# Attention mixed with a long convolution on one core: table exponentials ahead of the sines, a quarter of x transposed by DMA, operands padded to 128 rows, zero products, a new order

## The chip, the core and the metric

The kernel runs on one core of a Trainium2 chip. The metric is the device time of one execution in microseconds (us). The engines of the core each work through a queue of their own: TensorE (PE; its weight loads are listed as PEld), VectorE (DVE), ScalarE (ACT), GpSimd (POOL) and SyncE (SP). DMAs are issued from the queues of SP, ACT and POOL.

## The reference, cut to what matters

```python
x = A_x                                              # 1 x 2048 x 448, bf16
g = sigmoid((x * gate_w).sum(-1, keepdims=True))
q = heads(x @ wq)                                    # 16 heads of 28
k = x @ wk;  v = x @ wv                              # one head of keys and values for all
p = softmax(q @ k.T * 28 ** -0.5)                    # 16 x 2048 x 2048
a = join(p @ v) @ wo
dt = exp(log_dt)
P = exp(dt * (A_re + 1j * A_im) * arange(2048))      # 448 channels x 256 modes x 2048
K = einsum("dn,dnl,dn->dl", C, P, dt * B).real       # one filter of 2048 taps per channel
b = causal_convolution(x, K) + x * Dskip
return g * a + (1 - g) * b
```

## The kernel before, in words

**Attention.** Scores are computed transposed, 128 keys by 512 queries a tile, 1024 tiles in all. They go in sets of three tiles and two tiles in turn (410 sets). `qk` (in `main`) issues a set's score products, either with the tiles of three heads beside each other in TensorE's rows (`row`, L1260) or one whole-array product per tile against the masked copy qM (`full`, L1269). ACT takes the exponential of a whole set in one instruction (L1293), out of five of the eight PSUM banks into a ring of 15 tiles in SBUF. `pv` (L1311) multiplies four tiles with the values and sums in bank 6; a column of ones beside the values gives the softmax's denominators. After 64 tiles, `norm` divides, and after four such groups `outp` and `fold` add the gated result to O in SBUF.

**Convolution.** `prep_params` turns the parameters into tables: on ACT `dt` (L801), a half and a whole sine (L833, L836), and six table exponentials, one of A_re times dt (L845) and five of its multiples (L849, `mq`). `masters` and `tables` build, on DVE and per block of 32 channels, tables of powers (14 blocks); `kgen` makes the filter taps of a block by small products, and writes them to DRAM (KP). `tload` reads them back as Toeplitz blocks of 512 KB (224 loads on SP's queue, L1068), and `conv` multiplies them with x in the order of U (L1092).

**The front.** `loads` brings x in four quarters (two DMAs each), the weights with 112 rows, the parameters, four of them transposed by the DMA, A_re plain. `prep_x` transposes every quarter of x by 16 products with the identity (L665) in four PSUM banks, copies them out on ACT (L676) and DVE (L678), projects the keys (L684), takes their largest magnitude (L691), and copies the keys out on ACT (L694). From the magnitudes comes Wb (L721, L722), which shifts the scores; `qproj` projects the queries of one group (L891, L897, L900, L903). The first scores need all of that. `warm` products with the identity (L522) keep TensorE's clock. Quarters 1 to 3 of the transposed x are parked in DRAM (XS). U is filled by eight copies on POOL (L617) and one DMA that shifts it by 16 columns. O's zeros come by DMA from a zero tile (zO) once the transposed x that lies in O has been used.

**The order.** `Prog` collects all operations with their dependencies and an estimate of each one's duration, and `schedule` lays out every engine's queue by a greedy list rule: earliest start first, priorities `pr` next; before the first softmax exponential the longest chain to it (shifted by the hand-set RANK) decides. `after` adds edges that are only for the order: it places the table exponentials behind the softmax exponentials of sets 2, 4, 6, 8, 10 and 12 (pexp). TWICE repeats the score products of the first tile in two-tile sets from set 10 to 23. PSUM banks 5 and 7 are lent to everything that is not scores or value sums (POOL = (7, 5)).

Of the kernel before, what the change touches and what calls it, by code (L numbers as in the profile page):

```python
# [28 lines left out]
FLIP = (0, 2, 3, 4, 5)  # L29
# [8 lines left out]
SIN2PI = 6.2831850  # L38
SQ = 1.0 / math.sqrt(DH)
# [31 lines left out]
class Op:  # L71
    __slots__ = ("i", "eng", "fn", "ns", "lat", "deps", "pr", "lock", "unlock", "slot", "ndma",
                 "count", "vc", "end", "comm", "extra", "mode", "ni", "done", "waits", "sb", "tl", "tfree", "frees")


class Prog:
# [6 lines left out]
    BLOCK, FIRST, FETCH, IDLE, NEED = 256, 192, 5900.0, 3300.0, .015  # L83
    HALF = (21000.0, 32000.0, 1.8)
    HEAD = 0.4
    RANK = {142: -3000, 102: -1500, 107: 1500, 188: -700, 28: -1500, 23: -3000, 121: -3000, 33: 1500, 57: 1500, 93: -700, 181: -700}
    POOL = (7, 5)
    AHEAD = 1500.0
    SLACK = {"pe": 400.0, "dve": 150.0}

    def __init__(self, nc, es):
        self.nc, self.es = nc, es
        self.ops = []
        self.lastw = {}
        self.readers = {}
        self.slots = {}
        self.commops = {}
        self.after = {}
        self.convs = []

# [36 lines left out]
    def dma(self, pairs, desc, slot, rd=(), wr=(), pr=0, eng="sp", slow=False, extra=0, flip=False, cost=None):  # L137
# [11 lines left out]
        o.slot, o.ndma, o.extra = slot, len(pairs), extra  # L149
# [16 lines left out]
    def schedule(self):  # L166
# [27 lines left out]
        self.clock = {e: {} for e in ENG}  # L194
        block = [0.0, 0.0]
# [11 lines left out]
        while done < n:  # L207
# [53 lines left out]
            if e == "pool" and o.slot is None:  # L261
                for d in reversed(order[e]):
                    if ops[d].slot is None:
                        o.deps[d] = 1
                        break
            o.done = True
# [26 lines left out]
            if o.slot is not None:  # L293
                free[e] = r + self.ISSUE[e] * o.ndma
# [3 lines left out]
            else:  # L298
# [5 lines left out]
                if e == "pool":  # L304
                    held.append((r, free[e]))
            o.end = end
# [25 lines left out]
        return order  # L332

# [36 lines left out]
    def emit(self, block):  # L370
# [11 lines left out]
        for e in ENG:  # L382
# [3 lines left out]
            def body(x, e=e):  # L386
                for i in self.order[e]:
# [7 lines left out]
                    else:  # L395
                        r.then_inc(sem[e], 1)
                if e == "sp":
# [26 lines left out]
TWICE = 24  # L424


class Kernel:
# [26 lines left out]
    def alloc(self):  # L454
# [43 lines left out]
        self.XS = nc.dram_tensor("XS_scratch", (3 * DT * XQ,), BF).ap()  # L498
        self.R = nc.dram_tensor("R_scratch", (16 * 4 * 512,), F32).ap()

    def consts(self):
# [23 lines left out]
        self.warm = lambda n, b, ns: pg.op("pe", lambda e: warm(e, n, b), ns, rd=["id"], wr=[("b", b)], pr=-3)  # L525
# [3 lines left out]
        for _ in range(2):  # L529
            self.wd.append(len(pg.ops))  # L530
            self.warm(1, 3, 430)
        pm(V(self.Wm, 0, P), 0.0, 100, ["Wm"], 1)
# [20 lines left out]
    def loads(self):  # L553
# [4 lines left out]
        def lx(q):  # L558
            pg.dma([(bass.AP(tensor=self.xst.h, offset=h * self.xst.rs + q * 4 * D, ap=[[2 * self.xst.rs, 64], [D, 4], [1, D]]),
                     dram(x, (1024 * h + 256 * q) * D, [[D, 64], [64 * D, 4], [1, D]])) for h in range(2)],  # L560
                   (512, 896), f"x{q}", wr=[("xst", q)])
# [5 lines left out]
        def lraw(k):  # L567
            if k in FLIP:
                pg.dma([(raw.v(0, P, k * 1024, [[D, 2], [1, D]]), dram(ins[names[k]], 0, [[NM, D], [1, NM]]))],
                       (448, 512), f"raw{k}", wr=[("raw", k)], pr=0 if k < 2 else 0.2, flip=True, cost=1700)  # L570
# [13 lines left out]
        pg.dma([(wst.v(0, DT, 0, [[1, 4 * D]]), dram(ins["A_wq"], 0, [[4 * D, DT], [1, 4 * D]]))],  # L584
               (112, 3584), "wq", wr=["wqs"])
        pg.dma([(wks.v(0, DT, 112, [[1, 112]]), dram(ins["A_wv"], 0, [[112, DT], [1, 112]])),
                (wks.v(0, DT, 224, [[1, 4]]), dram(ins["gate_w"], 0, [[4, DT], [1, 4]]))],
               (224, 224), "wv", wr=["wvs"])
        lraw(1)
        pg.op("pool", lambda e: e.tensor_copy(self.Wk.v(0, DT, 0, [[32, 16], [1, DH]]),  # L590
                                             wks.v(0, DT, 0, [[DH, 4], [0, 4], [1, DH]])), 640, rd=["wks"], wr=["Wk"])
        pg.op("dve", lambda e: e.tensor_copy(self.Wq.v(0, DT, 0, [[512, NT], [32, 4], [1, DH]]),
                                             wst.v(0, DT, 0, [[16 * DH, NT], [DH, 4], [1, DH]])), 390, rd=["wqs", "Wq"], wr=["Wq0"], sb=True)
        pg.op("dve", lambda e: e.tensor_copy(self.Wq.v(0, DT, 128, [[512, NT], [32, 12], [1, DH]]),
                                             wst.v(0, DT, 4 * DH, [[16 * DH, NT], [DH, 12], [1, DH]])), 480, rd=["wqs"], wr=["Wq"], sb=True, pr=1)
        self.wvc = len(pg.ops)
        pg.op("dve", lambda e: e.tensor_copy(self.Wv.v(0, DT, 0, [[32, 4], [1, DH]]), wks.v(0, DT, 112, [[DH, 4], [1, DH]])),
              180, rd=["wvs"], wr=["Wv"], sb=True, pr=0.1)
        pg.op("dve", lambda e: e.tensor_copy(self.Wv.v(0, DT, 28, [[32, 4]]), wks.v(0, DT, 224, [[1, 4]])),
              100, rd=["wvs"], wr=["Wvg"], sb=True, pr=0.1)  # L600
# [12 lines left out]

        for q in range(4):
            for j in (0, 2):
                u = 15 - 4 * q - j
                pg.op("pool", lambda e, u=u: e.tensor_copy(  # L617
                    self.U.v(0, P, u - 1, [[32, D], [1, 2]]),
                    self.xst.v(0, P, (16 - u) * D, [[1, D], [-D, 2]])), 1080,
# [31 lines left out]
    def prep_x(self):  # L651
# [3 lines left out]
        for q in range(4):  # L655
            xT, xo = self.xq(q)
            t4, o4 = self.bank(4 + 2 * (q % 2))
            X = ("b", 4 + 2 * (q % 2))
            for T in (2, 0, 3, 1):
# [744 lines left out]
```

## Time and profile before

| | us |
|---|---|
| median of the runs shown (508.69, 508.8, 510.62) | 508.8 |
| the profiled execution | 507.82 |
| its span, first to last instruction | 505.8 |
| busy: ACT / DVE / PE / POOL | 485.6 / 451.6 / 451.5 / 163.7 |
| first softmax exponential starts | 20.61 |
| last softmax exponential ends | 497.99 |
| granted TensorE clock, mean | 0.959 |

The profile's page gives busy time by engine, the span in 40 slices with the granted clock (PEclk, in tenths of full speed), the costliest groups of instructions with the idle time ahead of them and what ended it, and the DMA issues. The trace behind it can be asked for a timeline of one engine, for the waits, and for busy time and clock in any stretch. A busy time says how full an engine is, not that it sets the end; what sets it is read from the idle time of the others ahead of their instructions.

### The profile page before, as it was taken

How to read it: one execution, taken by the hardware profiler on the slowest of the kernel's cores; microseconds unless marked ns; L12 is line 12 of the kernel's file. 1: busy time of each engine (PE TensorE's matmuls, PEld its weight loads, DVE VectorE, ACT ScalarE, POOL GpSimd, SP SyncE). 2: the span in 40 equal slices, each digit the busy share in tenths (PEclk: the TensorE clock that was granted, in tenths of full speed). 3: DMA queues.
4: the chain of work that ended last, by engine and by line, in shares of the span. 5: the costliest groups of instructions: out<-in, count | busy, mean ns of one | idle time of the engine just before them, and what ended most of it. 6: DMA issues, size and time to landing. Idle time of an engine off the chain costs nothing.

```text
span 505.8 us, 18926 instructions
## 1 busy us (share of the span) xinstructions
PE 451.5 (89%) x8474; PEld 197.9 (39%) x8474; DVE 451.6 (89%) x825; ACT 485.6 (96%) x438; POOL 163.7 (32%) x304
## 2 busy tenths in 40 slices
PE   8888788897889899989898999999898999999895
PEld 5413131342434344334344444343344443444463
DVE  7999999999999999999999999999999999423434
ACT  5999999999999999999999999999999999999883
POOL 8800223252233424215205525225133525051001
PEclk9959977999999999989999999999999999999988
DMA  8987408959889788988998999999996999999922
GB/s 209 238 65 117 98 7 246 346 185 318 299 267 309 231 281 266 359 296 257 371 296 241 348 358 305 340 366 292 358 324 231 373 374 372 370 372 386 361 74 45
DMA packets 115730, 138.45 MB, mean 274 GB/s; under 512 B 48841, under 2 KB 55402, under 8 KB 115650
## 3 DMA queue, kind: packets, MB, share of 16 engines
q1 hardware_dynamic: 105872, 127.82, 78.4%
q0 software_dynamic: 8768, 9.31, 7.0%
q8 instruction: 66, 1.08, 0.9%
q10 hardware_dynamic: 1010, 0.12, 0.2%
q14 instruction: 14, 0.11, 0.1%
HBM read 125.41 MB, written 5.22 MB: 258 GB/s over the span
## 4 chain that ended last, share of the span: by engine, by line
DVE 52%; ACT 34%; PE 10%; issue 2%; DMA 1%; SPq 1%
ACT expT L1293 33%; DVE tab L985 8%; DVE tab L997 5%; DVE tab L996 5%; DVE tab L1007 4%; DVE tab L994 4%; DVE tab L995 4%; DVE tmp L1003 3%; PE psS L1269 2%; PE psB L1311 2%; DVE msq L928 2%; DVE cst L1107 2%; PE psS L1260 2%; DVE seedz L932 1%; DVE mbf L948 1%
## 5 line engine op out<-in xcount | busy, mean ns | idle before, releaser
L1293 ACT ACTIVATE expT<-psS 128x1536 bf16<-128x1536 f32 (+1 forms) x410 | 466.6, 1338 | 6.4 <-PE psS L1260 4.1
L1269 PE MATMUL psS<-qM,kT 128*128 128x512 bf16 (+2 forms) x464 | 127.7, 370 | 13.0 <-ACT expT L1293 12.3
L1260 PE MATMUL psS<-qT,kT 29*128 29x512 bf16 (+2 forms) x702 | 86.1, 374 | 25.6 <-ACT expT L1293 22.2
L1311 PE MATMUL psB<-expT,vaug 128*32 128x512 bf16 (+2 forms) x1152 | 106.3, 378 | 0.4 <-issue 0.2
L143 POOL DMA_DIRECT2D KP_scratch<-kstg x112 | 61.6, 558 | 70.1 <-DVE kstg L1047 42.8
L985 DVE TENSOR_TENSOR tab<-tab,mbf 128x512 bf16<-128x512 bf16 (+3 forms) x56 | 64.5, 1153 | 0.0
L1311 PEld LDWEIGHTS psB<-expT,vaug 128*32 128x32 bf16 x1152 | 27.8, 94 | 79.3 <-issue 75.0
L143 POOL DMA_DIRECT2D rdenB<-R_scratch x56 | 28.5, 515 | 67.5 <-DMA R_scratch<-denT 46.8
L1260 PEld LDWEIGHTS psS<-qT,kT 29*128 29x128 bf16 x702 | 22.1, 92 | 71.2 <-ACT expT L1293 56.2
L1269 PEld LDWEIGHTS psS<-qM,kT 128*128 128x128 bf16 x464 | 30.2, 99 | 50.4 <-ACT expT L1293 33.4
L143 POOL DMA_DIRECT2D qM<-qT x64 | 32.2, 511 | 31.7 <-DVE qT L903 15.4
L996 DVE TENSOR_TENSOR tab<-tab 128x128 bf16<-128x128 bf16 (+4 forms) x70 | 41.8, 597 | 0.0
L997 DVE TENSOR_TENSOR tab<-tab 128x128 bf16<-128x128 bf16 (+4 forms) x70 | 41.6, 594 | 0.0
L1092 PE MATMUL psX<-T,U 128*32 128x128 bf16 (+3 forms) x1472 | 34.9, 222 | 0.8 <-issue 0.7
L1007 DVE TENSOR_TENSOR tab<-tab,tmp 128x4096 bf16<-128x4096 bf16 x14 | 31.9, 2278 | 0.1
L994 DVE TENSOR_TENSOR tab<-tab,mbf 128x4096 bf16<-128x4096 bf16 x14 | 32.0, 2285 | 0.0
L995 DVE TENSOR_TENSOR tab<-tab,mbf 128x4096 bf16<-128x4096 bf16 x14 | 31.9, 2280 | 0.0
L1092 PE MATMUL psS<-T,U 128*32 128x128 bf16 (+7 forms) x1248 | 29.6, 220 | 1.9 <-issue 1.0
L1092 PEld LDWEIGHTS psX<-T,U 128*32 128x32 bf16 (+3 forms) x1472 | 24.9, 94 | 13.6 <-issue 10.2
L143 POOL DMA_DIRECT2D denT<-acc x14 | 10.0, 716 | 60.8 <-DVE acc L1166 56.0
L1092 PEld LDWEIGHTS psS<-T,U 128*32 128x32 bf16 (+7 forms) x1248 | 20.4, 93 | 15.9 <-issue 11.9
L928 DVE TENSOR_TENSOR msq<-seedz 128x512 f32<-128x512 f32 (+3 forms) x50 | 26.2, 523 | 0.1
(164 smaller groups left out, 537.1 us busy)
## 6 DMA issues: line engine op xcount, KB each, us to landing
T<-KP_scratch SPq DMA_DIRECT2D x170, 512.0 KB, 8.6
U<-KP_scratch SPq DMA_DIRECT2D x40, 512.0 KB, 9.2
tab<-KP_scratch SPq DMA_DIRECT2D x14, 512.0 KB, 9.9
rdenB<-R_scratch POOLq DMA_DIRECT2D x56, 64.0 KB
qM<-qT POOLq DMA_DIRECT2D x64, 32.0 KB, 4.9
tab<-in_A_x_dram SPq DMA_DIRECT2D x8, 224.0 KB, 3.5
O<-cst SPq DMA_DIRECT2D x1, 1792.0 KB, 9.2
KP_scratch<-kstg POOLq DMA_DIRECT2D x112, 16.0 KB, 4.4
```

The costliest lines, as they stand in the source:

```text
L143: return [e.dma_start(o, i, **kw) for o, i in pairs]
L985: vo(lambda e, dst=dst, src=src, mri=mri: e.tensor_tensor(dst, src, mri, ALU.mult), 4 * n, done + mk(lv), [kr, ki, tk])
L994: vo(lambda e, src=src, mi=mi, tv=tv: e.tensor_tensor(tv, src, mi, ALU.mult), 2 * n, done + mk(lv), [tk])
L995: vo(lambda e, dst=dst, src=src, mr=mr: e.tensor_tensor(dst, src, mr, ALU.mult), 2 * n, done + mk(lv), [kr, ki, ("gap", s)])
L996: vo(lambda e, dc=dc, tc=tc: e.tensor_tensor(dc[0], dc[0], tc[1], ALU.subtract), n, [tk, kr], [kr])
L997: vo(lambda e, dc=dc, tc=tc: e.tensor_tensor(dc[1], dc[1], tc[0], ALU.add), n, [tk, ki], [ki])
L1007: vo(lambda e: e.tensor_tensor(tab.v(0, P, FM, [[4, 1024], [1, 4]]), tab.v(0, P, lo + 124, [[CG, 32], [-4, 32], [1, 4]]), rho.v(0, P, 0, [ ...
L1092: r = e.matmul(ps.v(32 * j, 32 - 2 * n, 128 * k, [[1, 128]]), self.U.v(0, P, (4 * gi + j) * 32 + 2 * n, [[1, 32 - 2 * n]]), tbuf.v(0, P, t ...
L1260: r = e.matmul(self.psS.v(0, P, 512 * b + o, [[1, n]]), kT.v(32 * h, DH + 1, 128 * kt, [[1, 128]]), qT.v(32 * h, DH + 1, 512 * (i % 2) + q ...
L1269: r = e.matmul(self.psS.v(0, P, 512 * b + o, [[1, n]]), kT.v(0, P, 128 * kt, [[1, 128]]), self.qM.v(0, P, (i % 2) * XQ + 512 * h + qo, [[1 ...
L1293: pg.op("act", lambda e: e.activation(expT.v(0, P, 512 * es[0], spread(es, n)), self.psS.v(0, P, 512 * bs[0], spread(bs, n)), AF.Exp, scal ...
L1311: r = e.matmul(self.psB.v(32 * h, 32, qo, [[1, n]]), vaug.v(0, P, 32 * kt, [[1, 32]]), expT.v(0, P, 512 * ring[t] + o, [[1, n]]), start=(k ...
```

## The change

- A_re is also transposed by the DMA (FLIP has 1), so its eight products and its PSUM group go. The six table exponentials stand ahead of the sines in ACT's queue, before the softmax begins; the sine table is loaded behind them, and the order edges pexp go.
- Quarter 2 of x comes transposed by two DMAs (DQ) from rows of 512 columns, of which 448 count; its 16 products and four copies go. It is also loaded plain, for U, behind the parameters, and its two copies into U stand behind the softmax exponentials of sets 6 and 11 (UF). Its columns have another order (`cols`), as have the reciprocals of its gate, now seven small ones for one.
- x, Wk, Wv, Wq and the gate's weights lie on 128 rows (three of 128 and one of 64, zeros below) instead of 112. Wk, Wv and the gate's weights are issued on ACT's queue, in two DMAs each.
- The transposes of x use two PSUM banks in place of four; the quarters go in the order 0, 1, 3, 2; fewer copies are on ACT (XA); the keys of quarter 0 are copied out on DVE (KD).
- Zero products: `idle` watches, while the order is made, how much of the last 3.4 us TensorE works, and where it is below 0.49 between 36 and 440 us puts products of the identity with a zero column into bank 6's sum (`filler`). There are 19 of them. TWICE goes from 24 to 40, three warm products follow each of the first four sets, and bank 5 is lent out after those.
- The scheduler's numbers change (HEAD, RANK, SLACK and others), some priorities, and with them the order on every engine.

```diff
-FLIP = (0, 2, 3, 4, 5)
+FLIP = (0, 1, 2, 3, 4, 5)
...
+XA = ((0, 1), (0, 3), (1, 3), (2, 1), (3, 1), (3, 2), (3, 3))
+KD = (0,)
+GX = 3
+DQ = (2,)
+NA, NB, ND = 4, 4, 4
+UF = range(6, 26, 5)[:2 * len(DQ)]
+QO = (0, 1, 3, 2)
...
-    POOL = (7, 5)
+    POOL = (7,)
+    LOW, SPAN, FILL = .49, 3413.0, (36000.0, 440000.0)
...
+    def idle(self, order, free, r, o):
+        a, span = self.act, self.SPAN
+        busy = sum(x for e, x in a[-60:] if e > r - span)
+        k = 0
+        if self.part < 15 and self.FILL[0] < r < self.FILL[1] and busy < self.LOW * span:
+            k = max(0, int(min((r - free - 60.0) / 218.0, (self.LOW * span - busy) / 215.0 + 1.0)))
...
-TWICE = 24
+TWICE = 40
...
+            if q in DQ and not y:
+                xT, xo = self.xq(q)
+                pg.dma([(xT.v(0, P, xo + 256 * h, [[512, 4], [1, 256]]), dram(x, (1024 * h + 256 * q) * D, [[D, 256], [1, 512]]))
+                        for h in range(2)], (1024, 512), f"w{q}", wr=self.xk(q), flip=True, cost=2500)
+                return
...
-        lx(0)
-        pg.dma([(wks.v(0, DT, 0, [[1, 112]]), dram(ins["A_wk"], 0, [[112, DT], [1, 112]]))], (112, 224), "wk", wr=["wks"])
-        lx(1)
-        lraw(0)
-        lx(2)
-        lx(3)
...
-        lraw(1)
+        lx(QO[0])
+        pg.dma(rows(wks, 0, ins["A_wk"], DH), (448, 56), "wk", wr=["wks"], eng="act", cost=150)
+        lx(QO[1])
+        lraw(1)
+        lraw(0)
+        pg.dma(rows(wst, 0, ins["A_wq"], D), (448, 896), "wq", wr=["wqs"], cost=1500)
+        lx(QO[2])
+        lx(QO[3])
+        pg.dma(rows(wks, 4 * DH, ins["A_wv"], DH), (448, 56), "wv", wr=["wvs"], eng="act", cost=150)
...
         def texp(e):
-            r = e.activation(dtp, d1, AF.Copy, scale=1.0 / TWO_PI)
-            e.preload_act_table(AF.Sin)
-            return r
+            return e.activation(dtp, d1, AF.Copy, scale=1.0 / TWO_PI)
...
+        pg.op("act", lambda e: e.activation(t(2), t(0), AF.Exp), 950, rd=[K(0)], wr=[K(2)], pr=-1)
+
+        def modulus(e, lv):
+            r = e.activation(self.mq.v(0, P, lv * W2, [[32, 2], [64, NC], [1, 32]]), tc(0), AF.Exp, scale=-2.0 * 2 ** lv)
+            if lv == 4:
+                e.preload_act_table(AF.Sin)
+            return r
...
-            for k, x in enumerate((2, 4, 6, 8, 10, 12)):
-                if s == x:
-                    pg.after[self.pexp[k]] = len(pg.ops) - 1
...
+            if s < ND:
+                x = len(pg.ops) - 1
+                for k in range(3):
+                    pg.after[len(pg.ops)] = x
+                    self.warm(1, 5, 218, 0.6)
...
+        pg.filler = lambda e: e.matmul(self.psB.v(0, P, 0, [[1, 512]]), self.ident.v(0, P, 0, [[1, P]]), vaug.v(0, P, 29, [[0, 512]]),
+                                       start=False, stop=True, tile_position=(0, 0), skip_group_check=True)
```

More of the change, by code (lines that the diff above doesn't have):

```diff
@@ L194, in schedule @@
         self.clock = {e: {} for e in ENG}
+        self.fill, self.act, self.part = {}, [], 15
         block = [0.0, 0.0]
@@ L265, in schedule @@
                         break
+            if e == "pe":
+                npe += 2 * self.idle(order[e], free[e], r, o)
             o.done = True
@@ L332, in schedule @@
         return order
+    def idle(self, order, free, r, o):
[4 more added lines that the diff above has]
+            k = max(0, int(min((r - free - 60.0) / 218.0, (self.LOW * span - busy) / 215.0 + 1.0)))
+        if k:
+            self.fill[order[-1]] = k
+            a.append((r, 215.0 * k))
+        a.append((r + o.ns, min(o.ns, 213.0 * o.ni / 8.0 if o.mode == "q" else o.ns)))
+        self.part = self.parts.get(o.i, self.part)
+        return k
     def clocks(self, o, order, tot):
@@ L396, in body @@
                         r.then_inc(sem[e], 1)
+                    for _ in range(self.fill.get(i, 0)):
+                        self.filler(x)
                 if e == "sp":
@@ L654, in prep_x @@
         sm = self.small
-        for q in range(4):
+        nb = 0
+        for iq, q in enumerate(QO):
             xT, xo = self.xq(q)
-            t4, o4 = self.bank(4 + 2 * (q % 2))
-            X = ("b", 4 + 2 * (q % 2))
-            for T in (2, 0, 3, 1):
-                b = (4 * q + T) % 4
+            t4, o4 = self.bank((4, 3, 2, 5)[iq])
+            X = ("b", (4, 3, 2, 5)[iq])
+            for T in (2, 0, 3, 1) if q not in DQ else ():
+                b = nb % 2
+                nb += 1
                 t, o = self.bank(b)
@@ L726, in prep_x @@
         self.q0 = q0 = [o.i for o in pg.ops[self.wb:] if o.eng == "dve"][-1]
-        pg.after[self.wvc] = pg.after[self.wvc + 1] = q0
+        pg.after[self.wqc] = q0
+        for k in range(NB):
+            pg.after[len(pg.ops)] = q0 - 1
+            self.warm(1, 3, 218, 0.6)
         self.q1 = len(pg.ops)
```

219 lines of the change are left out of this document (123 added, 96 removed).

## The prediction

> **What bounds the kernel now.** I read the page's busy shares first, then its clock row and its costliest groups, then ScalarE's (ACT) timeline, last the stretch table.
>
> ```profile
> PE 451.5 (89%) x8474; PEld 197.9 (39%) x8474; DVE 451.6 (89%) x825; ACT 485.6 (96%) x438; POOL 163.7 (32%) x304
> ...
> PEclk9959977999999999989999999999999999999988
> ...
> L1293 ACT ACTIVATE expT<-psS 128x1536 bf16<-128x1536 f32 (+1 forms) x410 | 466.6, 1338 | 6.4 <-PE psS L1260 4.1
> ```
>
> ACT is busy 96% of the span, 466.6 us of it with the 410 softmax exponentials, which this change keeps one for one. They form a stream from 20.61 to 497.99 us. So the span is four terms: the front before the first exponential (20.6), the exponentials, what else stands in their stream (idle 6.4, and other ACT work), and the end behind the last (505.8 - 498.0 = 7.8). Whoever wants time must take it from the front, the fill or the end.
>
> The fill, in ACT's timeline (start, duration, line, operation, idle before it):
>
> ```profile
> 19.46 0.69 ACT L694 ACTIVATE kT<-psS,small 128x512 bf16<-128x512 f32 x1
> 20.04 0.68 ACT L694 ACTIVATE kT<-psB,small 128x512 bf16<-128x512 f32 x1
> 20.61 3.70 ACT L1293 ACTIVATE expT<-psS 128x1536 bf16<-128x1536 f32 x3
> 24.17 0.98 ACT L845 ACTIVATE T<-T 128x896 f32<-128x896 f32 x1
> 25.01 1.05 ACT L1293 ACTIVATE expT<-psS 128x1024 bf16<-128x1024 f32 x1
> ...
> 27.31 1.01 ACT L849 ACTIVATE mq<-T 128x896 bf16<-128x896 f32 x1
> 28.15 2.42 ACT L1293 ACTIVATE expT<-psS 128x1024 bf16<-128x1024 f32 x2
> ```
>
> One table exponential (L845) and five like L849 stand among the softmax ones. Each pushes the next back by 0.84 (27.31 to 28.15): six times 0.84 = 5.0 us, directly on the bound. With the idle this closes the stream: 466.6 + 6.4 + 5.0 = 478.0 against 477.4 (neighbours overlap a little).
>
> The idle, from the same timeline: 0.26 at 38, then 0.33, 0.45, 0.15 and 0.43 between 66 and 86, 0.50 at 169, 0.22 and 0.57 at 220 to 222, 0.18 at 313, and 2.97 after 471. Most of it lies where TensorE's clock is granted at half (stretch, its length, busy PE, PEld, DVE, ACT, POOL, clock, DMA share, GB/s):
>
> ```profile
> 27.20:30.60 3.40, 2.19 (x17) 0.32 (x9) 3.40 (x8) 3.40 (x5) 0.00 (x0) 0.50 0.93 79
> ...
> 64.60:68.00 3.40, 2.88 (x48) 0.99 (x49) 3.23 (x13) 2.67 (x3) 0.57 (x1) 0.50 0.00 0
> 81.60:85.00 3.40, 3.40 (x18) 0.74 (x16) 3.40 (x5) 3.33 (x4) 0.00 (x0) 0.50 1.04 297
> ...
> 300.00:400.00 100.00, 93.56 (x2023) 41.75 (x2023) 99.83 (x181) 99.81 (x89) 34.09 (x63) 1.00 0.95 324
> ```
>
> Half clock alone costs ACT nothing (27 to 31: 3.40 of 3.40); with table products beside it, it does. The last row matters too: VectorE (DVE) is as full as ACT, so work added there is late at once, for the convolution though, not for ACT.
>
> **Part 1: six table exponentials out of the stream: -5.0.** They are not gone; the front has to hold them.
>
> **Part 2: the front, +2.7.** Before, ACT has four gaps ahead of 20.61, 1.26 + 0.85 + 0.23 + 0.64 = 3.0 us:
>
> ```profile
> 5.27 1.28 ACT L799 ACT_TABLE_LOAD   x1
> 6.56 1.08 ACT L676 ACTIVATE xT<-psS 112x512 bf16<-112x512 f32 x2
> 8.91 1.18 ACT L676 ACTIVATE T<-psS 112x512 bf16<-112x512 f32 x2 [1.26 <-PE psS L665]
> ...
> 17.19 0.95 ACT L836 ACTIVATE T<-T 128x896 f32<-128x896 f32 x1
> 18.16 1.28 ACT L837 ACT_TABLE_LOAD   x1
> ```
>
> The changed instruction order puts onto ACT: six weight loads to issue ahead of its first table load (Wk, Wv, gate), the six table exponentials, and the load of the sine table after them rather than at 5.27, where x was still on its way. It takes off four of ten x copies and one of four kT copies. Added up:
> - Six issues at 0.42 to 0.78 each (single issues on SP; ACT's own one takes 0.51), say 0.6: from 1.33 to 4.9. Table load 1.28, exponential 0.54, copy 0.58: 7.4. The casts of x's first quarter then start at 7.4, not 6.56.
> - The first table exponential needs A_re times dt on DVE, which stands behind a small copy (0.16) that waits for the gate weights, the last of those loads. Issued at about 4.3, landing after 2.7 (log_dt: 0.82 to 3.51) to 4.3 (gate weights before): 7.0 to 8.6. The copy, then 1.08: 8.3 to 9.9. I take 9.3.
> - From there ACT runs without a gap: six table exponentials 5.0, four x copies at 0.59 = 2.4, sine table 1.28, one kT 0.65, two sines 1.95, exponential table 1.28, two kT 1.26. Sum 13.8: the first softmax exponential at 23.2, bounds 22.2 and 25.5 (issues of 0.78 and the slow landing).
> - DVE's chain to the same point: after 9.4 its eighteen instructions up to the second qT cast, by their rows some 12.7 with their overlaps (the round of 1.81, the 1.34 before it, five reductions and two kT/qT casts of 0.68, four x casts, L853 1.05): 22.1, then 0.6 for the score product. Close behind ACT.
> - x's quarter by DMA transpose: two issues behind x's third load, the second from about 10.4. The four transposes of B and C land 3.6 to 4.5 after issue, so about 15. TensorE's queue stops there in order, with the first query product behind it, but the chain above needs these products only from 16.5. Cost 0; from a landing of 17 on it is one for one.
> - Two PSUM banks for the transposes instead of four: each round is cast 0.69, products 0.5, two hand-overs of 0.15. Six rounds from 5.0 end at 14, under the 23. Cost 0.
>
> So 23.3 against 20.6: **+2.7**, bounds +1.6 and +4.9.
>
> On the table loads, the trace: L837 starts 0.02 after the sine and lasts 1.28, and a copy starts 0.02 later. The Trainium skill (ScalarE: Activation LUTs, What ACT_TABLE_LOAD costs) gives 1.283 and a drain of 1.38 besides for every switch. By that rule the newly uncovered switch would cost 1.4 more, and the forecast below would be 505.9. The trace shows the 1.28 and no drain.
>
> **Part 3: keeping the clock, -2.0.** Score products of the first 40 sets repeated (8 more sets than before, two products each), 19 zero products into the value sum, three plain products after each of the first four sets. The 35 of the first two kinds take 0.21 each when back to back (three in a row last 0.82 in the records at 20.3, with an overlap): 7.5 us. TensorE is busy 41.0 of 50 in 50 to 100 and 90 of 100 afterwards, so they lie in its gaps: 0; uncovered, each holds back the scores, +7.5 at most. What they can win is the idle in half clock: 0.93 + 0.43 + 0.79 + 0.26 = 2.4. I take 2.0; the end's 2.97 is beyond their reach.
>
> The Trainium skill (TensorE: Matmul & The Clock Gate, Why this matters for your kernels) asks for no TensorE gap over about 3 us. By that rule nothing here could lose the clock, and this part is worth 0. The trace disagrees: the longest gap ahead of a product from 25 to 37 us is 1.14 and the clock is 0.50 all the while. So the share of work seems to count, which is what these products raise.
>
> **Part 4: the rest, 0.** DVE gains about 2 us (kT cast 0.68, seven small reciprocals for one at some 0.2 each, three memsets), and two copies of x on POOL move from the front to the sixth and eleventh set, where they may stretch DVE's work: L831 beside such a copy took 1.81, L853 of the same shape without one 1.05, so 0.8 each. Some 3.6 us later tables. What hides them: the last generator cast is at 442.10, while the last of 22 buffer loads after it issues at 471.7, at 1.35 each; the last eight need 11 us, so 15 us are to spare. XS writes, zO and the U shift now stand in another order on SP; the U shift landed in 22.5, and from about 38 it lands at 60, before the first buffer load at 77. The 128-row operands change no product's length (moving size 512 as before). The tail's 7.8 stays.
>
> **Sum.** Span 505.8 - 5.0 + 2.7 - 2.0 = 501.5; the execution takes 2.0 more than its span (507.8), so 503.5. The profiled execution stands 1.0 below the median, 508.8. Forecast **504.5**; its own range is 501.5 to 506.2. A measurement of this kernel can tell about 0.5% (2.5 us) from no change.
>
> **Rivals.**
> 1. *The front eats it*: the first exponential at 25.5 to 27 (late gate weights, or x's transposed quarter after 17) or no clock won: 506.3 to 510. For it: ACT's front has 3.0 us of gaps for 5.0 of work. Against: four copies leave it. At 25.5 with the clock term at 0 it is 508.8 - 5.0 + 4.9 = 508.7. The gap rule above gives the middle of this: 506.5.
> 2. *More falls away*: front at 22.2 and half of the end's idle gone too: 508.8 - 5.0 + 1.6 - 2.4 - 1.5 = 501.5, down to 498 with all idle. For it: the end's 1.43 before 478.43 stands beside one stall of 1.68 in TensorE's issue, which another order may not meet. Against: nothing in the change aims there.
> 3. *Slower: late convolutions stop TensorE's queue.* In the new order the first convolution's products stand 12.7 us of exponentials later than before, the last ones 2.7 later, with almost no score product behind them. TensorE takes its queue in order, so a buffer load that lands late holds scores behind it, and ACT with them. Now the last load lands at 480 and its products run at 488 to 494. With ACT some 4 us earlier 3.5 to 4 of that margin are left; each further us of delay in the loads is lost one for one, so the gain is gone at a slip of 8, and at 12 the time is 512. For it: DMA share 1.06 from 400 on, nothing to catch up with. Against: the 15 us above.
> 4. *It doesn't do what it says*: half clock comes back elsewhere and the front gives up what the stream gains; that lies in rival 1.
>
> **How the numbers follow.** Forecast 0.55, rival 1 0.22, rival 2 0.11, rival 3 0.12. Faster by over 0.5% (below 506.3): the forecast and rival 2, 0.66. Within: 0.22. Slower (above 511.3): 0.12. The range reaches to 499 (rival 2's middle) and to 510 (all of rival 1), leaving rival 3 and the rest of rival 2.
>
> **What would show it.** In the profile after: no table exponential between softmax ones; the first softmax exponential at 22 to 25.5; its idle column at 3 to 5; clock 1.00 in 63 to 86, still half somewhere before 40; last load on SP near 472; 7.8 behind the last exponential. I am wrong if the first exponential comes after 27, if ACT waits for scores whose products queue behind convolution products, or if the idle column grows.

## The result and the profile after

The changed kernel takes **516.4 us** (median of 6 runs, 514.69 to 519.23) against 508.9 for the kernel before on the same chip (508.69 to 510.62; 508.7 to 509.8 beside the later runs, 508.8 is used below): ratio 1.0134, 95% interval 1.0105 to 1.0164. That is slower by 1.3%, clear of the noise, where 504.5 had been forecast. Its profiled execution took 519.23 (span 517.4) and stands 2.9 above its median; that of before took 507.82 (span 505.8), 1.0 below its own. So the two profiles lie 11.4 us apart and the medians 7.6: of a shift read between these profiles, up to 3.9 us can be the choice of executions.

The page of the changed kernel, the lines that answer to those of before:

```profile
PE 435.7 (84%) x8389; PEld 197.5 (38%) x8496; DVE 454.8 (88%) x835; ACT 483.4 (93%) x433; POOL 166.4 (32%) x310
...
PEclk9999999999999999999999899899999999999997
...
L1357 ACT ACTIVATE expT<-psS 128x1536 bf16<-128x1536 f32 (+1 forms) x410 | 466.6, 1323 | 11.9 <-PE psS L1323 8.6
```

ACT has the same 466.6 us of softmax exponentials, but its idle column went from 6.4 to 11.9. The clock row lost its early dips and has small new ones in the 23rd and 26th slice (285 to 297 and 323 to 336 us).

ACT's timeline around the first softmax exponential (start, duration, line, operation):

```profile
23.27 1.26 ACT L750 ACTIVATE kT<-psS,small 128x512 bf16<-128x512 f32 x2
24.45 4.63 ACT L1357 ACTIVATE expT<-psS 128x1536 bf16<-128x1536 f32 x4
28.93 0.22 ACT L793 ACTIVATE gt<-psB 128x16 f32<-128x16 f32 x1
```

It starts at 24.45, not 20.61, and no table exponential stands behind it. The stretch table (length, busy PE, PEld, DVE, ACT, POOL, clock, DMA share, GB/s), the four stretches of before and one more:

```profile
27.20:30.60 3.40, 3.40 (x26) 0.89 (x24) 3.40 (x5) 3.40 (x5) 1.32 (x1) 1.00 0.39 90
64.60:68.00 3.40, 2.90 (x22) 0.81 (x19) 3.40 (x6) 3.40 (x4) 0.00 (x0) 1.00 0.00 1
81.60:85.00 3.40, 3.17 (x22) 0.97 (x22) 3.40 (x9) 3.40 (x4) 0.88 (x2) 1.00 0.96 328
300.00:400.00 100.00, 88.37 (x1841) 39.46 (x1868) 97.01 (x173) 97.03 (x87) 30.95 (x57) 0.98 0.92 310
320.00:340.00 20.00, 16.87 (x300) 6.71 (x303) 17.24 (x25) 17.05 (x16) 4.39 (x8) 0.91 0.93 307
```

The half clock is gone from the first three, as intended (and from 25 to 100 us as a whole: 0.82 before, 1.00 after). But from 300 to 400 DVE and ACT, both at 99.8 of 100 before, are at 97.0, and in the last row both lack about 3 of 20. When both full engines lose time together, look at what they share. Rows of all engines' timeline there:

```profile
327.32 2.60 ACT L1357 ACTIVATE expT<-psS 128x1536 bf16<-128x1536 f32 x2
...
328.25 0.31 PE L1181 MATMUL psS<-ident,cst 128*64 128x64 bf16 x7
...
330.85 0.35 PE L1181 MATMUL psS<-ident,cst 128*64 128x64 bf16 x9 [2.29 <-issue]
...
331.24 0.42 DVE L1189 TENSOR_TENSOR O<-O,psS 128x256 bf16<-128x256 bf16 x1 [1.89 <-PE psS L1181]
...
331.74 1.45 ACT L1357 ACTIVATE expT<-psS 128x1536 bf16<-128x1536 f32 x1 [1.82 <-PE psS L1323]
```

TensorE (PE) stops after the 7th of 16 identical small products, in the middle of one operation, where no wait stands; "issue" says that the profile knows no releaser. DVE and ACT then wait for products. What happened just before it goes on is in the DMA view of 328.2 to 329.4 us:

```profile
q8 instruction: 1, 0.02, 5.1%
```

One packet of queue q8, 16 KB; by the trace's records it starts at 328.32 and is there at 329.30, and TensorE runs on at 330.85. The queue has 66 such packets in each kernel and 67 in `a_shift32` below, whose TensorE queue is 64 instructions longer. The changed kernel has 17051 TensorE instructions (8496 weight loads, as many products, 59 others), some 256 for each packet: these are TensorE's own instructions. Such a **boundary stall** I count from the records as 0.6 us or more from the start of one TensorE instruction to the start of the next, after 100 us, at a 256-instruction boundary and ending 1.1 to 1.8 us after a q8 landing. Before had 4 of them, 5.1 us; the changed kernel has 10, 13.1 us.

The end, from the waits on SP's queue (waited for, us, times, longest), before and then after:

```profile
SPq L451 <- PEq L451: 1.4, 1, 1.4
```

```profile
SPq L483 <- PEq L483: 5.2, 1, 5.2
```

This is the barrier that closes the program. SP arrives with all output landed (504.2 before, 512.0 after), and the last to arrive is POOL, whose final drain ends at 505.57 and 517.17. POOL issues one output piece; its data landed at 511.54 in the changed kernel, 5.6 us ahead of the drain's end. The drain itself is about as long in both (496.98 to 505.57 before, 508.84 to 517.17 after). So the end hangs on the last addition of the convolution into O (496.24 before, 507.78 after; the span ends 9.6 behind it in both), not on the last softmax exponential, which ended 4.9 later than before.

The slip of 11.5 us in that addition begins in DVE's tables. The last block's table is ready at 446.85, before at 434.25: 12.6 later. The first block's is 3.4 later (the front), the second's 2.0. From there to the last block's, DVE's idle time is 8.1 us, before 0.9: 7.2 more. The remaining 3.4 is more work in that stretch (335.8 us busy against 332.4); 23 convolutions are added by then, before 22.

From the table the slip runs on almost unchanged. The last block's first taps are back in DRAM at 462.85, before at 449.63. SP waits for them, and from there its last 16 issues of Toeplitz loads follow each other with hardly a gap (0.04 us after most) to 483.79, before to 471.66: 20.9 and 22.0 us. The last of them in SP's timeline, before and then after:

```profile
465.07 6.59 SPq L1068 DMA_DIRECT2D T<-KP_scratch  x4
```

```profile
478.63 5.17 SPq L1131 DMA_DIRECT2D T<-KP_scratch  x4
```

### The profile page after: what moved, and what is told of

It is laid out like the page before. It is cut to its first block, busy times and chain, and to the rows that moved or that the text cites. A ratio compares the mean times of both kernels' runs of the same rounds, so it can differ in the third digit from the quotient of the medians.

```text
span 517.4 us, 18873 instructions
## 1 busy us (share of the span) xinstructions
PE 435.7 (84%) x8389; PEld 197.5 (38%) x8496; DVE 454.8 (88%) x835; ACT 483.4 (93%) x433; POOL 166.4 (32%) x310
## 3 DMA queue, kind: packets, MB, share of 16 engines
q8 instruction: 66, 1.08, 0.9%
## 4 chain that ended last, share of the span: by engine, by line
ACT 45%; DVE 33%; PE 15%; issue 3%; DMA 1%; SPq 1%; POOLq 0%; POOL 0%; DVEq 0%
ACT expT L1357 43%; DVE tab L1048 5%; PE psS L1332 3%; PE psB L1383 3%; DVE tab L1059 3%; DVE tab L1060 3%; PE psS L1323 2%; DVE tab L1057 2%; DVE tab L1070 2%; DVE tab L1058 2%; DVE tmp L1066 2%; DVE msq L991 1%; PE psS L1155 1%; PE psX L1155 1%; DVE cst L1170 1%
## 5 line engine op out<-in xcount | busy, mean ns | idle before, releaser
L1357 ACT ACTIVATE expT<-psS 128x1536 bf16<-128x1536 f32 (+1 forms) x410 | 466.6, 1323 | 11.9 <-PE psS L1323 8.6
L1332 PE MATMUL psS<-qM,kT 128*128 128x512 bf16 (+2 forms) x388 | 107.8, 357 | 27.8 <-ACT expT L1357 13.5
L1383 PE MATMUL psB<-expT,vaug 128*32 128x512 bf16 (+2 forms) x1152 | 104.4, 367 | 3.7 <-issue 2.9
L1323 PE MATMUL psS<-qT,kT 29*128 29x512 bf16 (+2 forms) x702 | 83.6, 364 | 21.6 <-ACT expT L1357 18.9
L154 POOL DMA_DIRECT2D qM<-qT x64 | 32.1, 510 | 31.9 <-DVE qT L966 16.6
L1155 PE MATMUL psS<-T,U 128*32 128x128 bf16 (+7 forms) x1408 | 35.2, 223 | 0.5 <-DMA T<-KP_scratch 0.3
L1155 PE MATMUL psX<-T,U 128*32 128x128 bf16 (+7 forms) x1312 | 32.2, 220 | 1.1 <-issue 1.1
L154 POOL DMA_DIRECT2D R_scratch<-denT x14 | 8.0, 570 | 72.5 <-DVE denT L1221 48.5
L1155 PEld LDWEIGHTS psS<-T,U 128*32 128x32 bf16 (+7 forms) x1408 | 24.2, 95 | 16.2 <-issue 11.1
L1155 PEld LDWEIGHTS psX<-T,U 128*32 128x32 bf16 (+7 forms) x1312 | 22.3, 94 | 13.7 <-issue 10.6
## 6 DMA issues: line engine op xcount, KB each, us to landing
T<-KP_scratch SPq DMA_DIRECT2D x170, 512.0 KB, 8.7
U<-KP_scratch SPq DMA_DIRECT2D x40, 512.0 KB, 9.0
tab<-KP_scratch SPq DMA_DIRECT2D x14, 512.0 KB, 10.9
```

The source lines that it names most:

```text
L154: return [e.dma_start(o, i, **kw) for o, i in pairs]
L1155: r = e.matmul(ps.v(32 * j, 32 - 2 * n, 128 * k, [[1, 128]]), self.U.v(0, P, (4 * gi + j) * 32 + 2 * n, [[1, 32 - 2 * n]]), tbuf.v(0, P, t ...
L1323: r = e.matmul(self.psS.v(0, P, 512 * b + o, [[1, n]]), kT.v(32 * h, DH + 1, 128 * kt, [[1, 128]]), qT.v(32 * h, DH + 1, 512 * (i % 2) + q ...
L1332: r = e.matmul(self.psS.v(0, P, 512 * b + o, [[1, n]]), kT.v(0, P, 128 * kt, [[1, 128]]), self.qM.v(0, P, (i % 2) * XQ + 512 * h + qo, [[1 ...
L1357: pg.op("act", lambda e: e.activation(expT.v(0, P, 512 * es[0], spread(es, n)), self.psS.v(0, P, 512 * bs[0], spread(bs, n)), AF.Exp, scal ...
L1383: r = e.matmul(self.psB.v(32 * h, 32, qo, [[1, n]]), vaug.v(0, P, 32 * kt, [[1, 32]]), expT.v(0, P, 512 * ring[t] + o, [[1, n]]), start=(k ...
```

## The experiments

Medians in us; "boundary stalls" as counted above, in the profiled execution. "Planned anew" means that the kernel's scheduler made a new order of all operations. The theory to test (theory 1): TensorE's next 256 instructions come late, DVE's tables and the convolutions slip with it, and POOL's ending stands open behind them. Rivals: 2, VectorE's added work and later start; 3, the products added to TensorE.

**The end.** `a_outz`, and the same edit on the kernel before, `b_outz`:

```
-        for k, e in enumerate(("pool", "act")):
+        for k, e in enumerate(("sp", "act")):
```

> The changed kernel with one edit: the next-to-last output piece (columns 416 to 447 of the first eight row blocks) is issued by SP, no longer by POOL; the plan's order is otherwise that of the changed kernel. Theory 1 (the end hangs on the last convolution's addition into O and then on POOL's own ending: in the profile of the changed kernel POOL's final drain ends at 517.2, 8.3 us after POOL's last DMA issue, while SP had seen the last output land by 512.0): the span ends at about 512.5, the time falls by some 5 us, to 511.5. Rival (the final drain follows the last landing whoever issues it, or the end is the last exponential plus 7.8 as the forecast had it): no change, 516 +- 1.

> The kernel before with the same one edit as a_outz (that output piece issued by SP, not POOL). Theory 1: in its profile POOL's ending came only 1.4 us behind SP's, so the time falls by 1 to 1.5 us, to 507.3: POOL's ending was hidden there and stood open in the changed kernel. Rival (issuing from POOL costs the same 5 us in any kernel): 503.8.

Measured: a_outz **511.5** (10 runs, 509.5 to 514.8; ratio to before 1.006, 1.0033 to 1.0087), b_outz **507.3** (10 runs; 0.9971, 0.9952 to 0.9990). Both as theory 1 had it, 4.9 and 1.5 us. The barrier's wait, in a_outz and in b_outz:

```profile
SPq L483 <- PEq L483: 0.2, 1, 0.2
```

```profile
SPq L451 <- PEq L451: 0.2, 1, 0.2
```

So 4.9 - 1.5 = 3.4 of the 7.6 us between the kernels (516.4 - 508.8) are POOL's ending: mostly hidden behind SP before, open once the convolution came late. 511.5 - 507.3 = 4.2 remain.

**The boundaries.** `a_shift32` and `b_shift32`: order untouched, 64 instructions put where TensorE idles anyway.

```
+                    for _ in range(32 * (e == "pe" and n == 0)):
+                        self.pad(x)      # one 128x1 product
                     r = o.fn(x)
```

> The changed kernel in exactly its order, with 32 one-column products (64 TensorE instructions) ahead of TensorE's first product, where it waits for x anyway. They move all later 256-instruction boundaries by 64 instructions and do nothing else. Theory 1: the stalls at 287, 331, 405, 412 and 488 us vanish or move to other places, and the time changes by over 2 us, up or down, with the sum of the stalls. Rivals 2 and 3 (VectorE's added work; products added to TensorE): within 1 us of 516.

> The kernel before in exactly its order, with the 64 TensorE instructions of a_shift32 ahead of its first product. If the places of the 256-instruction boundaries matter there as much as in the changed kernel, its stalls at boundaries (5.6 us, in the trace of before) grow to 12 to 20 us and the time to 514 to 520: then each plan is fitted to its own boundaries. If only the changed order is dense enough to be caught: 508 to 510.

Measured: a_shift32 **526.6** (1.035, 1.0296 to 1.0404), b_shift32 **525.4** (1.0318, 1.0272 to 1.0364). Shifting the boundaries costs 10.2 us in the changed kernel and 16.6 in the one before, the latter beyond its expected 514 to 520. Boundary stalls: 13.1 to 22.8 and 5.1 to 19.5, so 9.7 and 14.4 more. The ACT rows of the two, and the longest stall of a_shift32, from TensorE's timeline:

```profile
L1359 ACT ACTIVATE expT<-psS 128x1536 bf16<-128x1536 f32 (+1 forms) x410 | 466.8, 1340 | 21.3 <-PE psS L1325 15.8
```

```profile
L1295 ACT ACTIVATE expT<-psS 128x1536 bf16<-128x1536 f32 (+1 forms) x410 | 468.4, 1311 | 19.7 <-PE psS L1262 12.5
```

```profile
412.67 0.50 PE L1157 MATMUL psS<-T,U 128*28 128x128 bf16 x22
415.71 0.39 PE L1157 MATMUL psS<-T,U 128*18 128x128 bf16 x6 [2.53 <-issue]
```

Some product records are missing from the traces, but the weight loads are all there, one for each product, so the places can be counted by them. The stalls stand at one and the same place of every block, at instruction 192 + 256 k. The packet that ends a stall at the start of block k + 1 is the one that comes while TensorE works on block k. In a_outz it lands 4.4 us after TensorE has entered block k at the median (5.1 at the ninth decile, 6.3 at most), and in the stalls TensorE runs on some 1.4 us later. So a block that TensorE gets through faster than the sum, here 5.8 us, should end in a stall. From 390 to 480 us a block takes 6.2 to 6.4 us in both kernels: close to it.

**The cause of the late packets.** `b_small`, `a_small`, `b_small_shift`: the orders of b_outz, a_outz and b_shift32, with a quarter of each Toeplitz buffer loaded, the products reading that quarter again (the convolution's result is left out).

```
-  ap=[[2 * buf.rs, 64], [1024, 4], [1, 1024]]
+  ap=[[2 * buf.rs, 64], [1024, 4], [1, 256]]
...
-  tbuf.v(0, P, to + j * 1024 + 896 - 128 * n, [[1, 128]])
+  tbuf.v(0, P, to + j * 1024 + 128 * (n % 2), [[1, 128]])
```

> b_outz (the kernel before, that output piece issued by SP) in exactly its order, with a quarter of each Toeplitz buffer loaded (256 of 1024 columns; the products read these columns again, so the convolution's result is left out, while every product, cast and wait stays). The DMA engines then move about 50 MB instead of 139. Theory 1 (TensorE's next 16 KB of instructions land 4 to 7 us after they are asked for because they stand behind this traffic): the landing comes 1 to 2.5 us after the asking, the stalls at 256-instruction boundaries (5.6 us in the trace of before) go, and the time falls by 2 to 6 us below 507.3. Rival (the stalls have another cause, or cost nothing): 506 to 508.

> The same for the changed kernel: a_outz in exactly its order with a quarter of each Toeplitz buffer loaded. Theory 1: without boundary stalls (11.9 us in the trace of a_outz) the change's own gain comes out, that is the six table exponentials less the later front and the idle: the time falls by 6 to 12 us below 511.5 and lies 0 to 4 us below b_small. Rival 2 (VectorE's added work and later tables make it slower by themselves): it stays 3 us or more above b_small.

> b_small with the 64 TensorE instructions of b_shift32 in front. Theory 1: with the instructions there in time, the places of the boundaries stop mattering, within 1.5 us of b_small, where the same shift cost 16.6 us with full loads. Rival (the shift costs for another reason, such as the clock or the front): again 10 us or more above.

Measured: b_small **502.9** (0.9903, 0.9871 to 0.9935), a_small **501.7** (0.9873, 0.9839 to 0.9906), b_small_shift **503.8** (0.9897, 0.9859 to 0.9935). DMA and ACT rows of b_small, then ACT's of a_small:

```profile
DMA packets 116722, 50.37 MB, mean 101 GB/s; under 512 B 49865, under 2 KB 113770, under 8 KB 116642
...
L1293 ACT ACTIVATE expT<-psS 128x1536 bf16<-128x1536 f32 (+1 forms) x410 | 465.8, 1345 | 3.2 <-PE psS L1260 1.4
```

```profile
L1357 ACT ACTIVATE expT<-psS 128x1536 bf16<-128x1536 f32 (+1 forms) x410 | 465.3, 1320 | 3.5 <-PE psS L1323 2.4
```

With 101 GB/s of traffic in place of 270 the packets land 1.7 to 2.2 us after TensorE has entered the block (medians of the three). No stall of 0.6 us is left in b_small and a_small, and one of 0.62 in b_small_shift. The shift costs 0.9 us, not 16.6, and the changed kernel falls by 9.8 us. It ends 1.25 below the one before, though the two intervals overlap. Theory 1 is carried by this. One limit: the quarter loads also come sooner themselves, so the 9.8 us are not all instructions; the shift pair is free of that.

Rival 2 had the changed kernel 3 us or more above, and that is refuted. VectorE's part is not nothing, though. In a_small's profile the last table still comes 4.6 us later than in b_small's (438.3 against 433.7), without more idle time on DVE, and the last addition into O 6.2 later (498.5 against 492.3). So the stalls explain only part of the slip; how much of the 11.5 us stays without them is not known well, as a_small's profiled execution (504.5) stands 2.8 above its median.

**The parts, with stalls out of the way.** `a_p1_small` puts the table exponentials back between the softmax ones (sine table first again), `a_p3_small` takes the added products away (TWICE 24, no zero products, plain ones after one set). Both are planned anew.

> a_small with part 1 of the change undone (the six table exponentials go back between the softmax ones after sets 2 to 12, sine table loaded first), planned anew. With stalls out of the way it prices part 1 and 2 together: the forecast had -5.0 and +2.7 for them, the trace of the change shows the front 3.8 later. If the front is late because of these exponentials, the first softmax exponential comes at 20 to 21.5 here and the time is 1 to 2 us above a_small; if it is late for other reasons (weight loads issued by ScalarE, the gate weights), it comes at 23 or later and the time is 3 to 5 us above.

> a_small (changed kernel, output piece issued by SP, a quarter of each Toeplitz buffer loaded, so the convolution's result is left out) with part 3 undone: no zero products, score products repeated for 24 sets and not 40, plain products after the first set alone; planned anew. It prices the added products with TensorE's boundary stalls out of the way. The forecast's -2.0 says: granted clock back at half in parts of 30 to 90 us, idle ahead of the exponentials 2 us more than in a_small (3.5), time 503 to 504. If the products only cost, 500 or less; if they do nothing, 501 to 502.

Measured: 508.0 and 508.1, each some 6.4 above a_small. In a_p1_small the last exponential ends at 498.6, in a_small at 493.6: by these two profiles part 1 is worth 5.0, with its own cost in the front counted. That is rough, as the orders differ and a_small's profile stands 2.8 above its median. But the front barely moved; ACT's timeline of a_p1_small:

```profile
8.86 1.09 ACT L728 ACTIVATE xT<-psS 128x512 bf16<-128x512 f32 x2
12.80 0.60 ACT L728 ACTIVATE T<-psS 128x512 bf16<-128x512 f32 x1 [2.86 <-PE psS L718]
...
23.81 1.45 ACT L1355 ACTIVATE expT<-psS 128x1536 bf16<-128x1536 f32 x1 [0.22 <-PE psS L1321]
```

The first softmax exponential comes at 23.81 with the six moved out, and at 24.45 or 24.87 with them in (a_outz, a_small). ACT now waits, 2.86 for the second round of x. The median was above what I expected for a late front (3 to 5 us over a_small); the two profiled executions lie 3.1 apart.

a_p3_small missed too: 503 to 504 was expected, and 2 us more idle ahead of the exponentials, where it is 4.0 against 3.5. What the added products do shows between 25 and 100 us. Without them the granted clock is 0.76 from 30 to 50 and 0.83 from 70 to 90, with them 1.00 in both (from 25 to 30 it is 0.92 and 0.72). ACT is busy for 71.9 of the 75 us without them and for 74.0 with them, 2.1 more. The 370th exponential starts at 448.1 and 445.7, a difference of 2.4. The last one ends only 0.5 later (494.1 against 493.6). The convolution ends later (501.0 against 498.5 in the profiles), which goes with the new order; how the rest of the 6.4 comes about is open. Rival 3 finds no support: without the added products this kernel is slower, and so is a_nofill below.

**The front.** `a_nodq_o` (all of x transposed by TensorE) and `a_gate_o` (the copies of the value and gate weights behind A_re times dt), both on a_outz:

```
-DQ = (2,)
+DQ = ()
```

```
         vt(tt(0), p1, dtb, ALU.mult, [k1, "dt"], [K(0)], 0.2, unlock=p1)
+        pg.after[self.wvc] = pg.after[self.wvc + 1] = len(pg.ops) - 1
```

> The changed kernel with that output piece issued by SP, and with all four quarters of x transposed by TensorE (DQ empty), planned anew. The front is what it tells: first softmax exponential now at 24.45. If the transposed quarter is what makes it late, it comes at 23.5 or before; if the late gate weights and ScalarE's own work are, it comes at 25 to 26.5, since ScalarE and VectorE get four more casts. The total depends on the new plan's boundary stalls: 508 to 520.

> The changed kernel with that output piece issued by SP, and with VectorE's two small copies of the value and gate weights placed behind the product A_re times dt (planned anew). If the wait for the gate weights (2.1 us in the trace, the copy itself 0.80) is what delays the table exponentials, the first of them comes 1 to 2 us earlier than 12.0 and the first softmax exponential at 22.5 to 23.5. If ScalarE's own work is the bound, or the score's chain over VectorE, it stays at 24.2 or later. Total by the new plan's stalls, 508 to 520.

Measured: 514.5 and 512.1; first softmax exponential at 25.29 and 24.32, against 24.45. By these orders the transposed quarter wins 0.8, it does not cost. In a_gate_o the gate weights' wait is gone and the table exponentials start 1.08 earlier (10.91 before the edit), but the gain is used up on the way. Its ACT timeline:

```profile
9.83 0.95 ACT L892 ACTIVATE T<-T 128x896 f32<-128x896 f32 x1 [1.29 <-DVE T L888]
...
19.32 0.69 ACT L750 ACTIVATE kT<-psS,small 128x512 bf16<-128x512 f32 x1 [0.39 <-DVE small L742]
...
24.32 1.45 ACT L1358 ACTIVATE expT<-psS 128x1536 bf16<-128x1536 f32 x1
```

A copy of x (0.34, not shown) and then kT (0.39) wait now: x's products and DVE's reductions are as late as ACT.

**Other orders of the changed kernel.** The scheduler itself reckons with the boundaries: FETCH is the time in ns that it allows from entering a block to the start of the next, and NEED sets how far ahead of a boundary it holds less urgent products back. `a_fetch` gives it the two constants of the kernel before, `a_nofill` leaves out the zero products; both keep POOL's output piece.

```
-    BLOCK, FIRST, FETCH, IDLE, NEED = 256, 192, 5600.0, 3300.0, .02
+    BLOCK, FIRST, FETCH, IDLE, NEED = 256, 192, 5900.0, 3300.0, .015
```

```
-    LOW, SPAN, FILL = .49, 3413.0, (36000.0, 440000.0)
+    LOW, SPAN, FILL = .49, 3413.0, (0.0, 0.0)
```

> The changed kernel with two planner constants put back to those of the kernel before (FETCH 5600 to 5900, NEED .02 to .015), so that the plan spreads dense TensorE work further around the arrivals of its instruction blocks. Theory 1 (TensorE stood at 256-instruction boundaries for 1.2 to 2.5 us at 287, 331, 405, 412 and 488 us because its next 16 KB of instructions had not come, and the tables, loads and convolutions went late with it): most of these stalls go, idle ahead of the exponentials falls from 11.9 to about 8, the last convolution comes 4 to 8 us earlier, time 508 to 512. Rival 2 (the tables are late because VectorE has more work and starts later): 516 +- 1.5. Both plans differ in order, so a stall elsewhere may come in.

> The changed kernel without its 19 zero products into the value sum (the plan is made anew without them). Rival 3 (added products hold TensorE up): time 513 to 515, idle ahead of the exponentials below 11. Theory 1: the products as such are covered; only the places of the instruction boundaries change, time 514 to 518, with the granted clock unchanged or a little lower between 50 and 100 us.

Both missed: **518.9** and **524.7**. In a_fetch the stalls did shrink (13.1 to 7.5) and the last table came 12.1 earlier, at 434.7, close to the kernel before. But the generator's first product on it started 6.6 us behind the table (0.6 in the changed kernel), its result came 14.7 behind (8.5), and the last addition into O came at 508.0, 0.3 later than in the changed kernel. That the plan held these products back ahead of a boundary is not shown. a_nofill has the same gap, 14.6, and the addition at 513.2. So fewer stalls in all do not help where the last generator and convolutions come late.

`a_plan`, `a_plan2` (on a_outz) and `b_plan` (on b_outz): FETCH 6200, with NEED, AHEAD, the ranks and in b_plan HEAD changed too, as a search over the scheduler's own estimate of the span chose them.

> a_outz with nothing but the plan's constants changed: instruction blocks are counted as there 6.2 us after the asking (5.6 in the change; the trace of a_outz has 5.9 at the median from asking to running on), and the ranks are found anew by a search over the planner's own span. Theory 1 in the other direction: with full loads, an order that leaves TensorE more time per 256 instructions loses less at the boundaries than a_outz (11.9 us) and comes at 505 to 510, below 511.5. If the boundaries' landing times scatter too much to plan for, 511 to 518.

> A second order of the same kind for the changed kernel (same 6.2 us, other ranks, blocks spread over a longer stretch ahead of each boundary). Same expectation, 505 to 510; how far it lies from a_plan shows how much of a time is the luck of one order.

> b_outz (kernel before, output piece issued by SP) with the same treatment of its plan: 6.2 us in place of 5.9, other ranks. Its stalls at boundaries were 5.6 us, so less is to be had: 503 to 508 by theory 1, against 507.3; 508 to 515 if such an order is luck.

Measured: **510.3**, **509.8** and **517.0**, with boundary stalls of 6.3, 7.2 and 9.4 us. The changed kernel wins 1.2 and 1.7 us and is no slower than the kernel before (a_plan2: 1.0008, 0.9978 to 1.0038); a_plan just misses its range. b_plan, 9.7 above b_outz, lies beyond both of its ranges; 2.8 of that is already in the front (first softmax exponential at 23.70, in b_outz at 20.89). An order's time can so be planned only in part.

The fastest kernel with the full result is b_outz, the kernel before with one word changed (0.9971, 0.9952 to 0.9990).

## Why the prediction was wrong

The step that failed is **part 4, "the rest, 0"**, with its two supports: "15 us are to spare" behind the last generator cast, and "the tail's 7.8 stays". It had the tables some 3.6 us later, hidden by the spare time. They came 12.6 later, none of it was hidden, and the end behind the last exponential grew from 7.8 to 14.5. The new order was priced by what it moves on DVE, POOL and SP, not by what it does to TensorE's instruction supply.

- *What bounds the kernel.* "Front, exponentials, fill, end behind the last" has one chain. There are two, and the end belongs to the later one. Before, they ended close together (last exponential 497.99, last addition 496.24), and the 7.8 looked like a constant. After, the convolution's chain is last, and the end grew with it: 517.4 - 502.9 = 14.5 behind the last exponential. That POOL's drain closed before's span already was to be seen in its own waits (1.4 us).
- *The 15 us to spare* were not there in the trace of before either. The prediction took eight issues at 1.35 for the last block's loads. Each of these eight loads is two issues, and the 16 took 22.0 us. They could start only when the block's first taps had landed, 7.5 us after the cast had begun. That fills the time from 442.10 to 471.7, and a table 12.6 late gave a last load 12.1 late.
- *The sign of the stall.* Rival 2 had named the 1.68 us stall in TensorE's issue as something "another order may not meet". It was one of 4 boundary stalls; the other order meets 10.
- *Rival 3* had late convolutions, and a time of 512 at a slip of 12. The slip came (11.5 by the profiles), but the price was mainly another: the end itself, not scores queued behind late loads. Of the prediction's rivals this one came nearest.
- *Part 1, -5.0*: the stream gave that up as forecast: no table exponential stands in it any more. By the profiles of a_small and a_p1_small it is 5.0, net of what the six cost in the front.
- *Part 2, +2.7, bounds 1.6 and 4.9*: +3.8, within. ACT's issues ended at 5.07 (4.9 forecast), the first table exponential started at 10.91, 1.6 later than the 9.3 taken for it, and from there 13.5 us of work ran (13.8 forecast). What I had wrong is the reason: the six exponentials themselves cost the front only 0.6 to 1.1; 3.2 stay without them (23.81 against 20.61), since x and DVE's chain are as late.
- *Part 3, -2.0*: right in size (2.1 us of ACT's time between 25 and 100 us), and the clock came back where forecast, and before 40 us too, where half clock had been expected to stay.
- *The table load*: 17.18 plus 1.28, next work at 18.48. The drain of 1.38 that the Trainium skill adds (ScalarE: Activation LUTs, What ACT_TABLE_LOAD costs) is again not in the trace.

Up to the 247th exponential the sum held roughly: the 206th starts 1.3 us earlier than before (260.5 against 261.8), the 247th 1.3 later. The loss begins with the stalls at 287 and 331 us.

On the instruction supply, the Trainium skill (Runtime: NRT & Kernel Launch, Instruction fetch mechanics) says that the sequencer fetches 16 KiB blocks of 256 instructions over its own DMA queue while it executes the current one, and that crossing a block is "mostly hidden". The trace agrees on the blocks (66 packets of 16 KB) and disagrees on the hiding under this traffic: 13.1 us of stalls in the changed kernel, 22.8 in a_shift32, none in a_small at 101 GB/s.

What stays open: how the 4.2 us that remain without POOL's ending divide between the stalls and VectorE's later start and added work, and what each part is worth at full loads. Every edit of a part makes a new order, and orders of the changed kernel with POOL's ending taken out lie between 509.8 and 514.5 us; only the quarter-load kernels and the positions in the stream price the parts.

## What to carry to other kernels

Where a core's DMA queues are busy all the time (270 GB/s here), count the instructions of the busiest engine per microsecond. A run of 256 that takes less time than the next block needs to come (here some 5.8 us) is likely to end in a stall, and any edit ahead of it, even 64 idle instructions, moves all boundaries behind it. A time gained or lost by a reordering is not the reordering's own until the stalls in "issue" are compared. Look at who arrives last at the closing barrier before an end is called constant. And count issues, not loads, before time on a queue is called spare.

## What the runs showed of the hardware that I had not expected

- TensorE's instruction blocks land 4.4 us (median, a_outz) after the block before is entered at some 270 GB/s of traffic, and 1.7 to 2.2 us after at 101 GB/s; the same 64 instructions in front cost 16.6 us in the one case and 0.9 in the other.
- An output piece issued by POOL delays POOL's final drain to 8.3 us behind its last issue and 5.6 us behind its data's landing (508.84 to 517.17; landed 511.54). With the piece issued by SP, SP's wait at the closing barrier is 0.2, not 5.2.
